# Decode step with two layers: the first dense stage's queries and scores issued key head by key head, half of them as streamed rows

## The chip, the cores and the metric

The kernel runs on one core of one Trainium2 chip. The metric is device time in microseconds, the median of repeated executions. Before the change it is 269.35 us (median of 3 runs, 269.09 to 269.76). A program on the core is five instruction queues: TensorE (PE, with its weight loads shown apart as PEld), VectorE (DVE), ScalarE (ACT), GpSimd (POOL) and SyncE (SP). In this kernel SP does nothing but start DMA transfers, in order, and wait for the room that they need.

## The reference

Four tokens (B = 4, one position each) go twice through attention with a key/value cache and a gated feed-forward block. Cut to what matters:

```python
# D=512, Hq=32 query heads, Hkv=8 key heads, Sk=4096, Dh=128, F=1792, B=4
def attention(x, k_cache, v_cache, wq, wo):
    q = (x @ wq) as [B, Hq, Dh];  k, v repeated 4 times per key head
    p = softmax(q @ k^T * Dh**-0.5)
    return (p @ v) as [B, Hq*Dh] @ wo
def ffn(x, w_gate, w_up, w_down):
    return (gelu(x @ w_gate) * (x @ w_up)) @ w_down
for _ in range(2):
    x = x + attention(layernorm(x), ...)
    x = x + ffn(layernorm(x), ...)
```

Both layers use the same weights and the same caches. A cache tile is 2048 keys of one head of one token, 512 KB; there are 64 key tiles and 64 value tiles, the same for both layers.

## The kernel before, in words

The work goes token by token. `attend_first` does the first attention of token 0. Then, for each token b, the dense stage (out-projection, feed-forward), and then `attend`, which does the second attention of token b together with the first attention of token b+1, so that a tile in SBUF serves what it can. All orders are written out by hand (a manual schedule): each engine runs its instructions in the order of the program, and the framework adds only the waits. All loads go through SP's one queue, and a load is issued when its destination is free and when the transfer eight places earlier has landed.

The eight key heads form two groups of four (GH = 4), `gx` and `gy`; each head has a tile t = 0 and a tile t = 1 (`last`). For each group: queries are projected, "sums" matmuls by slices of the identity (`q_sums_of`, L326) bring them to a layout in PSUM (tile `qe`), DVE spreads them with masks into `qb` (`q_spread`, L334, the instruction at L337), and `scores_of` (L562, matmuls at L568) multiplies them with key tiles. One head's score matmuls write 32 partitions of the tile `sc`, so matmuls of four heads have four places side by side. `soft` (L573) makes the softmax: a reduction (L578), three small DVE steps, ACT's exponential (L590); then `soft_turn` (L596, L598) transposes on DVE, and DVE transposes the key tiles (`Keys.turn`, L513) for the next scores.

Special is the place after the first dense stage (b = 0), class `Early`. Key tiles of the previous attention are still in SBUF. Three first loads for the next token have gone to places that were emptied by copying ("parking") three old tiles elsewhere (L530); these are copied back (L541 on DVE, L544 on POOL, L546 on ACT) when score matmuls have freed other places. `Early.queries` (L1013) projects the 16 query heads of `gx` with matmuls that use weight blocks of `wq_sb` as stationary operand (L258, 4 per query head), into two accumulators in two PSUM banks: heads of key heads 2 and 3, then of 0 and 1. `q_round` (L310, L312) subtracts the mean and rounds to bf16. `Early.scores` (L1045) then runs the scores of `gx` in runs given to `first`, and calls `load` after each, which queues the next key tile for the place that this run frees. `rest` does sums and spread for key heads 0 and 1; `qy` (L1442) projects the 16 query heads of `gy` as streamed rows: 16 matmuls of 512 columns (L286), turned by DVE (L292) and rounded. `build`, called inside `soft`, does their sums and spread, with four matmuls of no use (`busy`, L465) that keep PE occupied.

Of the kernel before, what the change touches and what calls it, by code (L numbers as in the profile page):

```python
# [20 lines left out]
WIDE = 32  # L21
# [14 lines left out]
def kernel(  # L36
# [98 lines left out]
    def wide(v, width=WIDE):  # L135
        n = v.shape[-1]
        return v.unsqueeze(1).broadcast_to([P, width // n, n])
# [119 lines left out]
    def mac(dst, lhsT, rhs, first, last):  # L257
        nc.tensor.matmul(dst, lhsT=lhsT, rhs=rhs, start=first, stop=last, skip_group_check=True)  # L258
# [48 lines left out]
    def q_tile():  # L307
        return grp.tile([P, HG], BF16, name="q_bf", tag="q_bf", bufs=1)
# [9 lines left out]
    def q_sum_tile():  # L318
        return ps_sm.tile([P, GH, BE, rep], FP32, name="qe", tag="sm")
# [675 lines left out]
    class Early:  # L995
# [17 lines left out]
        def queries(self, b, st):  # L1013
            g, half = self.gx, GH // 2
            n = half * rep
            norm = Norm(st)
            norm.root()
            q_bf, qs = q_tile(), []

            def heads(h0, h1):  # L1020
                for i in range(h0, h1):
                    for k in range(KD):
                        mac(qs[-1][:, i % n], wq_sb[g][:, k, i * Dh:(i + 1) * Dh],
                            wide(xb[:, k, :RUN]), k == 0, k == KD - 1)

            qs.append(acc([n, WIDE], "q"))
            heads(n, 2 * n)
            q_round(q_bf, qs[0][:, :, b:b + 1], g, norm, n)
            qs.append(acc([n, WIDE], "q"))
            heads(0, n // 2)  # L1030
            qe = q_sum_tile()
            q_sums_of(qe, q_bf[:], half, half)
            heads(n // 2, n)
            q_spread(qe, half, half)
            q_round(q_bf, qs[1][:, :, b:b + 1], g, norm)

            def rest():
                q_sums_of(qe, q_bf[:], 0, half)
                q_spread(qe, 0, half)
                norm.scales()  # L1040

            self.rest = rest
            return norm

        def scores(self, sc, qy, norm):  # L1045
            gx, gy, own, keys = self.gx, self.gy, self.own, self.keys
            a, c, last = gx * GH, gy * GH, NT - 1

            def home(i, t, freed):
                place[i, t] = own[freed]  # L1050
                return k_tile(i, t).rearrange("p c d -> p (c d)")

            def load(i, t, freed):
                home(i, t, freed)
                assert keys.tile(keys.nl) == (i, t)
                keys.load(1)

            def first(run):
                now = {(a + s, t): place[a + s, t] for s, t in run}
                place.update({k: own[k] for k in now})  # L1060
                scores_of(sc, gx, run)
                place.update(now)

            first([(2, 0), (3, 0)])
            load(a + 3, 0, (a + 2, 0))
            load(a, last, (a + 3, 0))
            self.rest()
            q = qy()
            first([(2, last), (3, last), (0, 0), (1, 0)])
            load(a + 1, last, (a + 2, last))  # L1070
            load(a + 2, last, (a + 3, last))
            to = home(c + 1, last, (a + 1, 0))
            self.one.back(to, 1, nc.vector)
            self.one.back(to, 2, nc.gpsimd)
            self.two[0].back(home(c + 2, last, (a, 0)), 2)
            first([(0, last), (1, last)])
            load(a + 3, last, (a, last))
            to = home(c + 3, last, (a + 1, last))
            self.two[1].back(to, 1)
            other = new_scores()  # L1080

            def build():
                qe = q_sums(q)
                busy(4, other.rearrange("p c j -> p (c j)"))
                q_spread(qe)

            p0 = soft(sc, norm, meanwhile=build)
            self.two[1].back(to, 1, nc.vector)
            return p0, other

    def attend(b, qy, before, norm, early=None):

        gx, gy = second_groups[b - 1]
        prob1, prob2 = {}, {}
        keys = early.keys if early else Keys(b, (gx, gy))
        turn = keys.turn
        kept2, own2, other2, apart2 = two(b - 1)
        kept1, own1, _, apart1 = two(b)
        banks.late = len(apart2)
        vals2 = Values(2, b - 1, kept2 + own2 + apart2, prob2, dst2(b - 1),  # L1100
                       off_ot=len(apart2) > 0)
        late2 = Streamed(b - 1, other2, prob2, dst2(b - 1))
        vals1 = Values(1, b, one(b), prob1, dst1(b), keeps=kept1,
                       streamed=[gy * GH + s for s in range(GH - 1)], park=apart1,
                       sums={4: (ps_sc, "sc"), 5: (ps_sm, "sm"), 6: (ps_sc, "sc")},
                       last_bank=lambda: ps_sm.tile([P, 2, WEIGHT], FP32, name="ot", tag="sm"))

        sc2 = [new_scores(early=True)]
        if early:
            p0, other = early.scores(sc2[0], qy, norm)  # L1110
            sc2.append(other)
        else:
            for t in range(NT):
                scores(sc2[0], gx, t)
                keys.load_pairs(GH // 2)
            before.whole()
            p0 = soft(sc2[0], norm)
            q = qy()
            sc2.append(new_scores())
            busy(4, sc2[1].rearrange("p c j -> p (c j)"))  # L1120
            q_build(q)
        soft_turn(p0)
        ready = 2 if early else 0
        turn(ready)
        for t in range(NT):
            scores(sc2[1], gy, t)
            keys.load(GH)
        ring.extend(1, b, one(b)[ahead_of[b]:])
        ring.extend(2, b - 1, other2)
        ring.extend(2, b, own1)  # L1130
        pe0, den0 = soft_swap(p0, early=True), soft_den(p0)

        def recip():
            prob2[gx] = (pe0, soft_recip(den0))

        p1 = soft(sc2[1], norm, lasting=True, meanwhile=recip)
        vals2.step(2, hold=True)
        qe = q_sums(q1_bf[:, gx, :, b])
        vals2.step(4, hold=True)
        turn()  # L1140
        soft_turn(p1)
        q_spread(qe)
        vals2.flush()
        turn(1 if ready else 2)
        pe1, den1 = soft_swap(p1, early=True), soft_den(p1)
        banks.back_brief()
        banks.back()
        turn()
        prob2[gy] = (pe1, soft_recip(den1))
        turn(0 if ready else 1)  # L1150
        sc1 = new_scores()
        scores(sc1, gx, 0, singly)
        turn(3)
        scores(sc1, gx, 1, singly)
        turn()
        p0 = soft(sc1)
        vals2.step(vals2.left(), hold=True)
        turn()
        soft_turn(p0)
        q_build(q1_bf[:, gy, :, b])  # L1160
        vals2.flush()
        pe, den = soft_swap(p0), soft_den(p0)
        turn()
        prob1[gx] = (pe, soft_recip(den))
        turn()
        vals1.step(2)
        sc1 = new_scores()
        scores(sc1, gy, 0, last_alone)
        turn(4)
        vals1.step(3)  # L1170
        scores(sc1, gy, 1, last_alone)
        p0 = soft(sc1)
        vals1.step(3)
        x = swap_tile()
        busy(5, x.rearrange("p s t c h -> p (s t c h)"))
        vals1.put_aside(1)
        soft_turn(p0)
        vals1.put_aside(1)
        heads = pairs(one(b))
        twice = o1(b)  # L1180
        rows = RowProj(lambda i: twice(i).broadcast_to([P, 2]))
        pe, den = soft_swap(p0, x=x), soft_den(p0)
        vals1.put_aside(0)
        prob1[gy] = (pe, soft_recip(den))
        vals1.put_aside(0)
        vals1.step(2)
        rows.heads(heads[0], hp)
        vals1.step(2)
        rows.heads(heads[1], hp)
        vals1.step(1)  # L1190
        proj = OutProj(o1(b), 1)
        spare = proj.bank[:, KD * WEIGHT:]
        rows.heads(heads[2], rep)
        busy(3, spare)
        vals1.step(1)
        rows.heads(heads[2] + rep, rep)
        rows.split()
        busy(5, spare)
        vals1.step(1)
        proj.heads(heads[3], rep)  # L1200
        vals1.step(1)
        assert vals1.left() == 0
        rows.onto(proj)
        proj.n = Hq - rep
        proj.heads(heads[3] + rep, rep)
        return proj.y, late2
# [276 lines left out]
```

## Time and profile before

| | |
|---|---|
| median of 3 runs | 269.35 us (269.09 to 269.76) |
| the profiled execution, own time | 270.43 us |
| its span, first to last instruction | 268.7 us |
| PE busy | 199.4 us (74%) |
| PEld busy | 126.2 us (47%) |
| DVE busy | 176.4 us (66%) |
| ACT busy | 62.8 us (23%) |
| POOL busy | 3.9 us (1%) |
| DMA | 103.10 MB, mean 384 GB/s |
| mean granted TensorE clock | 0.898 |

How to read it: "busy" is the union of an engine's instructions over the span. The profile's second part cuts the span into 40 slices of 6.7 us and gives for each the busy share in tenths, the granted clock, the DMA share and the rate in GB/s. The chain is the work that ended last, followed back step by step. A timeline row has the start, the length, engine, line, operation, output<-input, and in brackets the idle time before it with what ended it. SPq is SP's queue, where a row is the issue of a transfer and not the transfer.

### The profile page before, as it was taken

The numbers are of one execution on the slowest core, as the hardware profiler recorded it, in microseconds if no ns is written. First come the engines' busy times: TensorE is split into PE (matmuls) and PEld (weight loads), VectorE is DVE, ScalarE is ACT, GpSimd is POOL, SyncE is SP. The second block draws the span as 40 slices with busy tenths as digits, with TensorE's granted clock in tenths as the row PEclk, the third lists the DMA queues.
The fourth block names the chain that finished last, engine by engine and source line by source line (L and its number), as shares of the span: only waits on it lengthen the run. The fifth ranks groups of instructions, "written<-read, shape, count | busy, mean of one in ns | idle before, by whom it ended". The sixth has DMA issues, their size and how long they took to land.

```text
span 268.7 us, 9239 instructions
## 1 busy us (share of the span) xinstructions
PE 199.4 (74%) x4104; PEld 126.2 (47%) x4113; DVE 176.4 (66%) x434; ACT 62.8 (23%) x123; POOL 3.9 (1%) x10
## 2 busy tenths in 40 slices
PE   1395255679689796979689867697699687978884
PEld 1333133568366544547346244364372344654563
DVE  3393952150226899884768997736779986468863
ACT  1001000200404402032315320304235203044630
POOL 2000000000001000000000000000000000000001
PEclk9999559559799978699999988999999977799999
DMA  6999999999996999999999999999999999999940
GB/s 248 420 417 420 417 420 418 413 381 401 409 401 212 396 416 420 417 417 417 395 412 418 417 420 417 417 420 381 395 420 416 417 420 417 417 356 358 417 161 3
DMA packets 32575, 103.10 MB, mean 384 GB/s; under 512 B 2836, under 2 KB 8728, under 8 KB 32536
## 3 DMA queue, kind: packets, MB, share of 16 engines
q1 hardware_dynamic: 32512, 102.51, 95.8%
q8 instruction: 32, 0.52, 0.7%
q14 instruction: 7, 0.06, 0.1%
q10 hardware_dynamic: 24, 0.01, 0.0%
HBM read 102.50 MB, written 0.00 MB: 382 GB/s over the span
## 4 chain that ended last, share of the span: by engine, by line
DMA 44%; PE 26%; DVE 20%; SPq 5%; ACT 2%; issue 2%; DVEq 0%
DMA v_t<-in_A_v_cache_dram 25%; DVE kp L513 11%; DMA kp<-in_A_k_cache_dram 9%; PE sc L568 7%; PE ot L824 6%; DMA wu_sb<-in_B_w_up_dram 5%; DMA kp<-in_A_v_cache_dram 4%; SPq L149 4%; PE y L258 3%; PE so L757 2%; PE u L258 1%; ACT pe L626 1%; PE q L286 1%; DVE pe L578 1%; DVE q L292 1%
## 5 line engine op out<-in xcount | busy, mean ns | idle before, releaser
L513 DVE STREAM_TRANSPOSE kp<-kp 128x1024 f32<-128x1024 f32 x64 | 74.0, 1207 | 0.0
L568 PE MATMUL sc<-kp,qb 128*32 128x512 bf16 x512 | 62.5, 432 | 6.6 <-DVE kp L513 2.2
L824 PE MATMUL ot<-pe,v_t 128*128 128x32 bf16 (+1 forms) x1120 | 37.3, 183 | 16.2 <-DMA v_t<-in_A_v_cache_dram 14.1
L824 PEld LDWEIGHTS <-v_t 128*128 128x128 bf16 x1120 | 34.4, 100 | 25.6 <-DMA v_t<-in_A_v_cache_dram 19.5
L568 PEld LDWEIGHTS <-qb 128*32 128x32 bf16 x512 | 21.8, 100 | 37.4 <-issue 19.3
L590 ACT ACTIVATE pe<-sc,nl 128x512 bf16<-128x512 f32 x8 | 5.5, 687 | 85.5 <-DVE pe L587 76.9
L765 DVE STREAM_TRANSPOSE so<-so 128x256 f32<-128x256 f32 (+1 forms) x19 | 11.1, 586 | 6.1 <-PE so L757 6.1
L623 PE MATMUL x<-pe,ident_bf 128*32 128x128 bf16 x192 | 5.8, 247 | 12.4 <-DVE pe L598 12.2
L258 PEld LDWEIGHTS <-wo_sb 128*128 128x128 bf16 x256 | 12.9, 99 | 3.5 <-DMA wo_sb<-in_A_wo_dram 2.9
L258 PE MATMUL y<-OT_bf,wo_sb 128*128 128x64 bf16 x192 | 11.7, 215 | 2.4 <-DMA wo_sb<-in_A_wo_dram 2.2
L623 PEld LDWEIGHTS <-ident_bf 128*32 128x32 bf16 x256 | 5.4, 102 | 17.1 <-issue 14.8
L578 DVE TENSOR_REDUCE pe<-sc 128x1 f32<-128x512 f32 x12 | 8.3, 690 | 6.3 <-PE sc L568 6.3
L656 DVE TENSOR_TENSOR OT_bf<-ot,rden 128x8 bf16<-128x8 f32 (+1 forms) x20 | 3.0, 156 | 13.5 <-PE ot L824 13.4
L626 ACT CAST pe<-x 128x512 bf16<-128x512 f32 x12 | 7.0, 585 | 20.4 <-PE x L623 20.4
L258 PE MATMUL q<-xb,wq_sb 128*128 128x5 bf16 (+1 forms) x192 | 5.5, 170 | 7.5 <-DMA wq_sb<-in_A_wq_dram 7.5
L757 PE MATMUL so<-v_t,pl 128*32 128x256 bf16 x192 | 9.2, 275 | 2.5 <-DMA v_t<-in_A_v_cache_dram 2.5
L401 DVE TENSOR_TENSOR xb<-XX,y 128x4 bf16<-128x4 f32 (+1 forms) x9 | 1.6, 173 | 13.7 <-PE y L258 13.5
L465 PEld LDWEIGHTS <-ident_bf 128*128 128x128 bf16 x131 | 7.5, 100 | 6.3 <-issue 3.4
L757 PE MATMUL so<-v_t,pe 128*32 128x256 bf16 x192 | 8.9, 303 | 2.1 <-ACT pe L626 1.1
L598 DVE STREAM_TRANSPOSE pe<-pe 128x512 bf16<-128x512 bf16 x12 | 8.4, 697 | 2.0 <-ACT pe L590 2.0
L330 PE MATMUL qe<-q_bf,ident_bf 128*32 128x16 bf16 (+1 forms) x272 | 5.5, 175 | 5.6 <-DVE q_bf L312 2.8
L258 PEld LDWEIGHTS <-wq_sb 128*128 128x128 bf16 x192 | 5.2, 98 | 8.1 <-DMA wq_sb<-in_A_wq_dram 8.1
(152 smaller groups left out, 252.9 us busy)
## 6 DMA issues: line engine op xcount, KB each, us to landing
v_t<-in_A_v_cache_dram SPq DMA_DIRECT2D x97, 512.0 KB, 8.9
kp<-in_A_k_cache_dram SPq DMA_DIRECT2D x56, 512.0 KB, 10.4
wq_sb<-in_A_wq_dram SPq DMA_DIRECT2D x2, 2048.0 KB
wo_sb<-in_A_wo_dram SPq DMA_DIRECT2D x4, 1024.0 KB, 11.4
kp<-in_A_k_cache_dram SPq DMA_DIRECT2D x4, 1024.0 KB, 8.7
wq_sb<-in_A_v_cache_dram SPq DMA_DIRECT2D x3, 1024.0 KB, 12.0
wg_sb<-in_B_w_gate_dram SPq DMA_DIRECT2D x1, 1792.0 KB, 12.5
wu_sb<-in_B_w_up_dram SPq DMA_DIRECT2D x1, 1792.0 KB
```

Source lines behind the costliest of these rows:

```text
L149: dq.dma_start(out=wo_sb[:, i * n:(i + 1) * n], in_=wo_dram[:, i * n:(i + 1) * n])
L258: nc.tensor.matmul(dst, lhsT=lhsT, rhs=rhs, start=first, stop=last, skip_group_check=True)
L465: nc.tensor.matmul(unread, lhsT=ident_bf[:], rhs=rhs[:, :unread.shape[1]], start=start, stop=start, skip_group_check=True)
L513: nc.vector.transpose(out=words, in_=words)
L568: nc.tensor.matmul(sc[s * QS:(s + 1) * QS], lhsT=qb[:, w0:w0 + 2 * W], rhs=kt[:, :, be // 2, :, be % 2], start=(t == 0 and be == 0), stop= ...
L578: nc.vector.tensor_reduce(out=m, in_=sc.rearrange("p c j -> p (c j)"), axis=AX.X, op=ALU.min if norm else ALU.max)
L598: nc.vector.transpose(out=flat, in_=flat)
L623: nc.tensor.matmul(x[a * QS:(a + 1) * QS, s], lhsT=ident_bf[:, s * QS:(s + 1) * QS], rhs=pT[:, a], start=True, stop=True, skip_group_check ...
L626: nc.scalar.copy(out=pe, in_=x.rearrange("p s t c h -> p (s t c h)"))
L757: nc.tensor.matmul(ps[d, :NW * QS], lhsT=x[:, w:w + NW].rearrange("p c h -> p (c h)"), rhs=v[:, i:i + NW, d], start=first and i == 0, stop ...
L765: nc.vector.transpose(out=flat, in_=flat)
L824: nc.tensor.matmul(self.ot[:, s % 2], lhsT=v[:, i, :], rhs=wide(pe[:, s, t * CH + i, :], self.ot.shape[-1]), start=(done == 0 and i == 0), ...
```

## The change

Only `Early.queries`, `Early.scores` and their call are touched.

In `queries`, all 16 query heads of `gx` get one accumulator of 512 columns (one PSUM bank). The heads of key head 2 and those of key head 3 are projected and rounded one key head after the other, and their sums and spreads are issued one key head at a time. The projections by weight blocks of key heads 0 and 1 (32 matmuls) are gone; `other_rows` makes these eight query heads as 16 streamed-row matmuls of 256 columns, and `other_half` turns and rounds them, and does their sums and spread. `norm.root` comes after the first spreads.

In `scores`, the runs of `first` are: (2,0) alone; (2,last) with (3,0); (3,last) alone; (0,0) with (1,0); (0,last) with (1,last). Before they were (2,0) with (3,0); then four together; then (0,last) with (1,last). The loads stand behind the new runs. `other_rows` stands ahead of the run (3,last); `other_half`, the rows of `gy` and their rounding stand ahead of (0,0),(1,0); the sums of `gy` stand ahead of (0,last),(1,last) and its spread, in two halves, behind. One `busy` matmul remains of four. `qy` is no longer called here.

```diff
@@ -1014,35 +1014,33 @@
             g, half = self.gx, GH // 2
             n = half * rep
             norm = Norm(st)
+            q_bf, qe = q_tile(), q_sum_tile()
+            q = acc([2 * n, WIDE], "q")
+            for s in range(half, GH):
+                for h in range(s * rep, (s + 1) * rep):
+                    for k in range(KD):
+                        mac(q[:, h], wq_sb[g][:, k, h * Dh:(h + 1) * Dh], wide(xb[:, k, :RUN]),
+                            k == 0, k == KD - 1)
+                q_round(q_bf, q[:, s * rep:(s + 1) * rep, b:b + 1], g, norm, s * rep)
+            for s in range(half, GH):
+                q_sums_of(qe, q_bf[:], s, 1)
+                q_spread(qe, s, 1)
             norm.root()
-            q_bf, qs = q_tile(), []
-
-            def heads(h0, h1):
-                for i in range(h0, h1):
-                    for k in range(KD):
-                        mac(qs[-1][:, i % n], wq_sb[g][:, k, i * Dh:(i + 1) * Dh],
-                            wide(xb[:, k, :RUN]), k == 0, k == KD - 1)
-
-            qs.append(acc([n, WIDE], "q"))
-            heads(n, 2 * n)
-            q_round(q_bf, qs[0][:, :, b:b + 1], g, norm, n)
-            qs.append(acc([n, WIDE], "q"))
-            heads(0, n // 2)
-            qe = q_sum_tile()
-            q_sums_of(qe, q_bf[:], half, half)
-            heads(n // 2, n)
-            q_spread(qe, half, half)
-            q_round(q_bf, qs[1][:, :, b:b + 1], g, norm)
-
-            def rest():
+
+            def other_rows():
+                steps = [(x, w[:, :n * Dh]) for x, w in q_steps(b, g)]
+                streamed_part(q[:, :n], steps, range(KD))
+
+            def other_half():
+                q_round(q_bf, turn_rows(q[:, :n]), g, norm)
                 q_sums_of(qe, q_bf[:], 0, half)
                 q_spread(qe, 0, half)
                 norm.scales()
 
-            self.rest = rest
+            self.other_rows, self.other_half = other_rows, other_half
             return norm
 
-        def scores(self, sc, qy, norm):
+        def scores(self, sc, b, norm):
             gx, gy, own, keys = self.gx, self.gy, self.own, self.keys
             a, c, last = gx * GH, gy * GH, NT - 1
 
@@ -1061,30 +1059,33 @@
                 scores_of(sc, gx, run)
                 place.update(now)
 
-            first([(2, 0), (3, 0)])
+            first([(2, 0)])
             load(a + 3, 0, (a + 2, 0))
+            first([(2, last), (3, 0)])
             load(a, last, (a + 3, 0))
-            self.rest()
-            q = qy()
-            first([(2, last), (3, last), (0, 0), (1, 0)])
             load(a + 1, last, (a + 2, last))
+            self.other_rows()
+            first([(3, last)])
             load(a + 2, last, (a + 3, last))
+            self.other_half()
+            raw = q_rows(b, gy)
+            q_bf, half = q_tile(), GH // 2
+            q_round(q_bf, turn_rows(raw), gy, norm)
+            first([(0, 0), (1, 0)])
             to = home(c + 1, last, (a + 1, 0))
             self.one.back(to, 1, nc.vector)
             self.one.back(to, 2, nc.gpsimd)
             self.two[0].back(home(c + 2, last, (a, 0)), 2)
+            qe = q_sums(q_bf[:])
             first([(0, last), (1, last)])
+            q_spread(qe, half, half)
             load(a + 3, last, (a, last))
             to = home(c + 3, last, (a + 1, last))
             self.two[1].back(to, 1)
             other = new_scores()
-
-            def build():
-                qe = q_sums(q)
-                busy(4, other.rearrange("p c j -> p (c j)"))
-                q_spread(qe)
-
-            p0 = soft(sc, norm, meanwhile=build)
+            q_spread(qe, 0, half)
+            busy(1, other.rearrange("p c j -> p (c j)"))
+            p0 = soft(sc, norm)
             self.two[1].back(to, 1, nc.vector)
             return p0, other
 
@@ -1107,7 +1108,7 @@
 
         sc2 = [new_scores(early=True)]
         if early:
-            p0, other = early.scores(sc2[0], qy, norm)
+            p0, other = early.scores(sc2[0], b - 1, norm)
             sc2.append(other)
         else:
             for t in range(NT):

```

## The prediction

> **What bounds the kernel now.** I read the page's rates by slice and its chain first, then SP's waits, then the stage that the change touches, row by row.
>
> ```profile
> GB/s 248 420 417 420 417 420 418 413 381 401 409 401 212 396 416 420 417 417 417 395 412 418 417 420 417 417 420 381 395 420 416 417 420 417 417 356 358 417 161 3
> DMA 44%; PE 26%; DVE 20%; SPq 5%; ACT 2%; issue 2%; DVEq 0%
> ```
>
> 103 MB have to come in, and nearly every slice runs at 395 to 420 GB/s: the span is the transfers plus a start and a tail. The one hole is slice 13 (80.6 to 87.3 us) at 212, and it is the changed stage. Seen closer, in stretches of 1 us (the last number is GB/s):
>
> ```profile
> 81.00:82.00 1.00, 1.00 (x40) 0.81 (x39) 0.47 (x2) 0.05 (x1) 0.00 (x0) 1.00 0.46 188
> 82.00:83.00 1.00, 1.00 (x32) 0.64 (x31) 0.05 (x1) 0.00 (x0) 0.00 (x0) 1.00 0.12 49
> 83.00:84.00 1.00, 1.00 (x26) 0.71 (x20) 0.59 (x4) 0.00 (x0) 0.00 (x0) 1.00 0.29 53
> ...
> 125.00:130.00 5.00, 4.00 (x132) 2.59 (x128) 3.75 (x14) 3.19 (x5) 0.00 (x0) 1.00 1.00 393
> ```
>
> SP's waits tell why: it stood 8.4 us at one key load, put down to PE, until the first run of scores had freed a place.
>
> ```profile
> SPq L494 <- PE qe L330: 8.8, 2, 8.4
> ```
>
> So an earlier first load is worth its full length, as long as nothing behind it gets late. Behind it is the second thing to see, the chain of this stretch: it is all compute from 78 to 114 us, DVE without a pause from 89 (5.00 us busy of 5 in 95 to 100), and the chain meets a transfer again at 114.
>
> ```profile
> 85.71 1.94 ACT kp L546 x2
> 87.64 0.77 ACT pe L590 x2
> 88.42 0.02 issue
> 88.44 0.58 DVE pe L598
> 89.02 0.06 issue
> 89.08 2.33 DVE kp L513 x2
> ...
> 114.00 6.94 DMA v_t<-in_A_v_cache_dram
> ```
>
> The softmax's exponential (87.52) waits for ACT's three copies, and these wait for the scores of heads 0 and 1.
>
> **The change, step by step.** Prices come from these rows:
>
> ```profile
> 79.74 1.35 PE L258 MATMUL q<-xb,wq_sb 128*128 128x32 bf16 x48
> 80.73 0.22 DVE L312 SCALAR_TENSOR_TENSOR q_bf<-cs_q,ln,q 128x8 bf16<-128x8 f32 x1 [0.21 <-PE q L258]
> 81.02 0.27 PE L330 MATMUL qe<-q_bf,ident_bf 128*32 128x8 bf16 x16
> 81.37 0.29 DVE L337 TENSOR_TENSOR qb<-qe,masks 128x128 bf16<-128x128 f32 x1 [0.41 <-PE qe L330]
> 81.71 0.63 PE L568 MATMUL sc<-kp,qb 128*32 128x512 bf16 x4
> ```
>
> A projection matmul lasts 0.176 and follows the last by 0.025; 16 sums take 0.27; a round of score matmuls starts 0.233 after the last one whether one, two or four places are filled, and lands 0.39 after its start. Hand-overs are 0.08 (PE to DVE), 0.07 and 0.05 (DVE to PE).
>
> 1. *First load.* Head 2's 16 projections end at 80.29, its rounding at 80.53. The compiled order of the changed kernel marks the first projection of head 3 as waiting for DVE, and so the first sum of head 3, while the score matmuls of (2,0) behind it carry no wait of their own. I read this as follows: PE may not write the query bank while DVE reads it, nor the sums' bank while DVE spreads. Then the heads do not overlap: projections of head 3 80.60 to 81.15, rounding to 81.39, head 2's spread 81.40 to 81.64 (0.24, an estimate from 0.29 for 128 columns and 0.41 for 256), head 3's sums from 81.70, scores (2,0) from 81.82 in four lone rounds to 82.91. The load goes at 82.94, and went at 82.84: **+0.1**. If head 3 need not wait, the same sum gives 82.37: **-0.45**. These are the two ends; I take +0.1, because the marked waits say so.
>
> The Trainium skill, "PSUM — Partial Sum Buffer", in its section on bank collisions, speaks against the change: two engines must not touch one bank in the same 32 partitions at once, even at other columns, so waits go by bank. Before, the halves had a bank each; no run here has yet shown the shared case. By the page the sum is +0.1, without it -0.45.
>
> 2. *The other loads.* (2,last) and (3,0) run 82.75 to 83.85: loads at 83.88 and 84.30 (83.27 and 84.73 before). Streamed rows end at 84.31 (four rounds of half of 0.216 each), (3,last) at 85.24: load at 85.27 (85.15).
>
> 3. *Heads 0 and 1 are late.* Before, their spread was ready at 83.33. Now: transpose of 256 columns 0.46 (the so row of that size at L765), rounding, sums, spread, ready at 85.78; the 16 rows of gy (0.87 before, all ahead of the scores in PE's queue) run 85.26 to 86.30. Scores (0,0),(1,0) run 86.13 to 87.22, and before were done at 84.71: **+2.5**. As a check: 12 rounds of scores become 20, so 8 x 0.233 = 1.9; 32 projections less give back 0.8, rows of 256 columns cost 0.43, and the rest is the DVE round trip.
>
> 4. *What hangs on it.* ACT's copies start 2.5 later (84.80 to 87.31). DVE: turn of gy 86.35, rounding to 87.34, the copy back to 88.07 (0.69), two spreads to 88.68; PE's gy sums wait for that rounding, so (0,last),(1,last) end at 88.62; then reduction and three small steps to about 90.2. Exponential at 90.3 and not 87.52: **+2.75**. Scores of gy start at 88.73 (86.66). Loads six and seven go at 88.65 and 89.82 (85.62 and 87.75). Three busy matmuls less win nothing: PE waits there anyway. Root and scales have room to the exponential.
>
> 5. *Out to the stream.* DVE has no pause from 89 to 112, so +2.75 arrives at 114. The next waits of PE for value tiles, at 120.98 and 122.27, give back some 0.5: the dense stage of token 1 is **+2.3**. Does this matter, when the stream is the bound? It does once loads come so late that too little is queued. Bytes issued less bytes landed, read from the trace at each issue, are 3.9 us of transfers at 110.38, 4.1 at 114.00, 3.7 at 118.19, and only 2.6 at 125.62; then 2.6 to 3.4 until 135. The chain shows one of these: 5.94 us from issue at 127.87 to the end of the wait. A lone transfer needs 2.7 to 3.3 us from issue to landing (the load of 82.84 landed at 85.57 to 86.10). So transfers of 1.25 us need about 3.5 us between issue and mean landing. With issues 2.3 late, those of 125.62 to 134.29 (4.1 to 5.1 from issue to mean landing before, so 0.6 to 1.6 spare) get short by 0.7 to 1.7, less some 0.3 where a wait of PE for a tile goes away (0.44 at 130.97). At 110 and 118 I count 0.5 to 0.9, which is the same lateness and not added. Between 0.7 and 1.7 I take 1.2, and 0.1 from step 1: **+1.3 us**. After 135 the queue holds 7 to 9 us again, and PE waits for tiles at 155 to 176, so the compute's lateness dies there and the stream's stays.
>
> The Trainium skill, "DMA: Bandwidth & Descriptors", section on the anatomy of one DMA, gives a fixed 2.0 us plus bytes at 436 GB/s, 3.2 us for a tile (fitted on another issue path). The 2.7 to 3.3 here is near; with 3.2 for 3.5 the sum would be +1.0.
>
> The profiled execution took 270.43 (268.7 span and 1.7 around it), so it would take 271.7; it lies 1.1 above the median of the runs, so the median goes from 269.35 to **270.65**.
>
> **The rivals.** About 0.3% (0.8 us) is what a measurement of this kernel can tell from no change.
>
> - *A, forecast:* late compute eats the queue's lead. +0.8 to +2.0, 270.1 to 271.4. Chance 0.58.
> - *B, the queue covers it:* the late compute costs nothing since 2.6 us are queued at the thinnest place; only the restart counts, +0.1 to +0.6, 269.65. For it: no slice between 90 and 230 falls below 381 now. Against it: at 2.6 us queued, 125 to 130 already runs at 393. Chance 0.20.
> - *C, faster:* head 3's projections do not wait, the first load goes at 82.37 (-0.45), and the late compute, then some 2.2, is covered. The earlier queue can also win part of what 84 to 90 lose now with little queued (315, 279, 326 and 391 GB/s against 417: 1.1 us): -0.9, 268.45. It decides where the first load is issued before 82.6 and over 1.5 us stay queued at 126. Against it: the marked waits. Chance 0.08.
> - *D, the whole lateness:* the chain from 78 to 114 is all compute; if the stream waits for every late issue, 2.75 less 0.5 stays: +2.3, 271.6. For it: the chain. Against it: 4.1 us queued at 114. Chance 0.14.
>
> **How the numbers follow.** A and D are slower by over 0.3%, except A's low edge (0.02); B is no change; of C 0.06 is faster and 0.02 is not: faster 0.06, same 0.24, slower 0.70. The range leaves out C and the upper half of D, 0.15 in all: 269.3 to 271.8.
>
> **What would show it.** First load near 82.94 and not 82.4 (step 1); head 3's projections after a pause of 0.3 at 80.3; ACT's first copy near 87.3 and the exponential near 90.3 (steps 3, 4); rates of 125 to 140 below 393 to 408 (step 5). I am wrong if those rates hold (B), if the first load is early (C), or if PE's clock, 1.0 from 75 to 90 now, drops in the new pauses, which I leave out.

## The result and the profile after

The changed kernel is slower. Its median is 273.0 us (6 runs, 270.74 to 275.92) beside 269.56 for the kernel before on the same chip (269.09 to 271.17): ratio 1.0102, 95% interval 1.0067 to 1.0138, or +1.8 to +3.7 us. Timed a second time, unchanged (x13 below), it gave 1.0071 (1.0045 to 1.0096). Both fit +1.8 to +2.6 us. The ratios here leave out executions more than 1.5% above the fastest of their kernel: the 275.92 among these six, and three of the twelve of x12. The first profiled execution took 272.78 (span 271.0, mean clock 0.884), the second 272.01 (270.2, 0.899), and that of before 270.43.

The rates by slice and the engines' shares of the chain, from the page of the changed kernel:

```profile
GB/s 253 420 418 420 418 420 417 409 383 404 406 389 183 288 399 418 417 408 390 394 398 418 418 417 415 423 415 404 391 415 416 417 421 417 418 384 393 417 164 3
DMA 45%; PE 23%; DVE 19%; SPq 8%; issue 2%; ACT 1%; DVEq 0%
```

The hole in slice 13 (183) is deeper than before (212), and slice 14 has become a second hole (288 for 396). Slices 18 to 21 (408 390 394 398) are the next dense stage, a little slower than 417 417 395 412. Slice 36 went the other way, 384 for 356. SP's longest wait in the stage is now for scores and 0.5 longer (8.4 before; the three numbers are the total in us, how often, and the longest):

```profile
SPq L494 <- PE sc L568: 16.7, 9, 8.9
```

The stage itself, in the timeline of the changed kernel; the brackets hold the idle time ahead of a row and what ended it:

```profile
79.57 0.55 PE L258 MATMUL q<-xb,wq_sb 128*128 128x32 bf16 x16
80.16 0.22 DVE L312 SCALAR_TENSOR_TENSOR q_bf<-cs_q,ln,q 128x4 bf16<-128x4 f32 x1 [0.25 <-PE q L258]
80.43 0.55 PE L258 MATMUL q<-xb,wq_sb 128*128 128x32 bf16 x16 [0.31 <-DVE q_bf L312]
...
81.53 0.26 PE L330 MATMUL qe<-q_bf,ident_bf 128*32 128x4 bf16 x16 [0.36 <-DVE qb L337]
81.66 2.05 PE L568 MATMUL sc<-kp,qb 128*32 128x512 bf16 x8
83.31 13.03 SPq L494 DMA_DIRECT2D kp<-in_A_k_cache_dram  x13
...
88.58 2.84 ACT L546 COPY kp<-park 128x1024 bf16<-128x1024 bf16 x3 [5.64 <-PE sc L568]
91.63 0.78 ACT L590 ACTIVATE pe<-sc,nl,ln 128x512 bf16<-128x512 f32 x1 [0.20 <-DVE pe L587]
```

Both pauses that step 1 read from the marked waits are there: PE stood 0.31 until DVE had rounded head 2's queries out of the shared bank, and 0.36 until DVE had spread out of the sums' bank. But the first load went at 83.31 and the exponential at 91.63, later than forecast (the dense stage ended 0.17 earlier here than in the trace of before). The windows of this trace say why; the number behind the five busy times is the granted clock:

```profile
81.00:82.00 1.00, 0.64 (x34) 0.41 (x35) 0.57 (x3) 0.00 (x0) 0.00 (x0) 0.97 0.48 197
82.00:83.00 1.00, 1.00 (x7) 0.36 (x5) 0.38 (x3) 0.41 (x2) 0.00 (x0) 0.50 0.11 33
83.00:84.00 1.00, 1.00 (x14) 0.35 (x12) 0.00 (x0) 0.00 (x0) 0.00 (x0) 0.50 0.00 0
84.00:85.00 1.00, 1.00 (x15) 0.38 (x14) 0.00 (x0) 0.00 (x0) 0.00 (x0) 0.50 0.49 131
```

From 82 to 85.4 PE had half its clock: rounds of score matmuls start 0.43 us apart there, and 0.22 apart in the second profile of the same kernel, which had no such stretch:

```profile
82.00:83.00 1.00, 1.00 (x14) 0.72 (x14) 0.48 (x3) 0.36 (x2) 0.00 (x0) 1.00 0.16 57
83.00:84.00 1.00, 1.00 (x22) 0.69 (x17) 0.00 (x0) 0.05 (x1) 0.00 (x0) 1.00 0.08 16
84.00:85.00 1.00, 0.73 (x14) 0.14 (x12) 0.69 (x2) 0.00 (x0) 0.00 (x0) 1.00 0.85 270
```

There the timeline is the forecast one. Its dense stage ended 0.06 earlier than that of before, so add 0.06 to compare: first load 82.88 (forecast 82.94), ACT's copies 87.05 (87.31), exponential 90.15 (90.3).

```profile
80.54 0.55 PE L258 MATMUL q<-xb,wq_sb 128*128 128x32 bf16 x16 [0.31 <-DVE q_bf L312]
...
82.82 11.66 SPq L494 DMA_DIRECT2D kp<-in_A_k_cache_dram  x13
...
86.99 2.84 ACT L546 COPY kp<-park 128x1024 bf16<-128x1024 bf16 x3 [3.94 <-PE sc L568]
...
90.09 0.78 ACT L590 ACTIVATE pe<-sc,nl,ln 128x512 bf16<-128x512 f32 x1 [0.26 <-DVE pe L587]
```

So the second profile is the one to account by. Where the bytes were lost, in windows of before and then of the second profile (last number GB/s):

```profile
86.00:88.00 2.00, 1.93 (x25) 0.63 (x28) 1.77 (x7) 2.00 (x3) 0.03 (x1) 1.00 0.91 326
88.00:90.00 2.00, 1.69 (x31) 0.77 (x28) 1.56 (x2) 1.05 (x4) 0.00 (x0) 1.00 1.02 391
90.00:92.00 2.00, 0.96 (x32) 0.94 (x32) 2.00 (x4) 0.25 (x1) 0.00 (x0) 1.00 1.03 408
92.00:95.00 3.00, 2.38 (x96) 2.19 (x96) 2.86 (x11) 1.18 (x3) 0.00 (x0) 0.99 1.02 407
130.00:135.00 5.00, 3.73 (x100) 1.94 (x92) 3.39 (x14) 0.41 (x2) 0.00 (x0) 1.00 1.02 406
```

```profile
86.00:88.00 2.00, 1.77 (x36) 0.64 (x30) 1.76 (x4) 1.01 (x2) 0.95 (x2) 1.00 0.77 242
88.00:90.00 2.00, 1.91 (x24) 0.55 (x20) 1.49 (x7) 1.83 (x3) 0.22 (x1) 1.00 1.01 410
90.00:92.00 2.00, 1.33 (x32) 0.55 (x29) 1.66 (x5) 1.18 (x3) 0.00 (x0) 1.00 0.93 332
92.00:95.00 3.00, 1.70 (x65) 1.47 (x52) 2.97 (x6) 0.59 (x1) 0.00 (x0) 1.00 0.97 300
130.00:135.00 5.00, 3.52 (x112) 2.14 (x105) 3.42 (x12) 2.03 (x3) 0.00 (x0) 1.00 0.95 320
```

From 86 to 95, 2 x 84 - 2 x 19 + 2 x 76 + 3 x 107 = 603 KB less arrive, 1.45 us at 417 GB/s. From 130 to 135 it is 5 x 86 = 430 KB, 1.0 us. What the stream lost in this profile it lost at these two places and a little between 115 and 125 us: it is 1.45 late at its 36th MB, still 1.7 at its 46th, and 2.9 at its 54th (138 us in the kernel before). The rest of the account is in the page of the second profile:

```profile
GB/s 251 422 416 420 419 418 418 410 382 403 408 392 202 338 403 417 417 407 409 338 401 418 416 417 419 415 420 397 398 415 419 416 419 418 418 399 395 419 149 3
```

Slices 36 and 37 (236 to 250 us) run at 399 and 395, before at 356 and 358: 80 GB/s over 6.75 us is 540 KB, **1.3 us won back** at the end.

### The profile page after: what moved, and what is told of

Its sections match the earlier page's. It is cut to its first block, busy times and chain, and to the rows that moved or that the text cites. A ratio compares the mean times of both kernels' runs of the same rounds, so it can differ in the third digit from the quotient of the medians.

```text
span 271.0 us, 9246 instructions
## 1 busy us (share of the span) xinstructions
PE 202.2 (75%) x4110; PEld 125.4 (46%) x4110; DVE 177.0 (65%) x438; ACT 62.9 (23%) x123; POOL 3.9 (1%) x10
## 4 chain that ended last, share of the span: by engine, by line
DMA 45%; PE 23%; DVE 19%; SPq 8%; issue 2%; ACT 1%; DVEq 0%
DMA v_t<-in_A_v_cache_dram 25%; DMA kp<-in_A_k_cache_dram 12%; DVE kp L513 10%; PE sc L568 7%; PE ot L824 5%; DMA kp<-in_A_v_cache_dram 4%; SPq L149 4%; DMA wd_sb<-in_B_w_down_dram 4%; SPq L154 3%; PE y L258 3%; PE so L757 2%; PE q L286 2%; DVE q L292 1%; DVE pe L578 1%; SPq L150 1%
## 5 line engine op out<-in xcount | busy, mean ns | idle before, releaser
L568 PE MATMUL sc<-kp,qb 128*32 128x512 bf16 x512 | 67.4, 443 | 5.9 <-DVE kp L513 1.9
L568 PEld LDWEIGHTS <-qb 128*32 128x32 bf16 x512 | 23.2, 102 | 38.8 <-issue 20.8
L578 DVE TENSOR_REDUCE pe<-sc 128x1 f32<-128x512 f32 x12 | 8.3, 689 | 5.9 <-PE sc L568 5.9
L258 PE MATMUL q<-xb,wq_sb 128*128 128x5 bf16 (+1 forms) x160 | 4.8, 169 | 7.8 <-DMA wq_sb<-in_A_wq_dram 7.5
L286 PE MATMUL q<-wq_sb,xb 128*32 128x512 bf16 (+1 forms) x128 | 10.0, 380 | 0.3 <-DVE xb L401 0.3
L292 DVE STREAM_TRANSPOSE q<-q 128x512 f32<-128x512 f32 (+1 forms) x8 | 5.6, 697 | 7.0 <-PE q L286 7.0
L757 PE MATMUL so<-v_t,pe 128*32 128x256 bf16 x192 | 8.0, 274 | 2.8 <-ACT pe L626 1.4
```

Source lines behind the costliest of these rows:

```text
L286: nc.tensor.matmul(flat[j * QS:(j + 1) * QS], lhsT=x.broadcast_to([P, WIDE]), rhs=blocks[:, j], start=i == 0, stop=i == len(steps) - 1, sk ...
L292: nc.vector.transpose(out=flat, in_=flat)
L568: nc.tensor.matmul(sc[s * QS:(s + 1) * QS], lhsT=qb[:, w0:w0 + 2 * W], rhs=kt[:, :, be // 2, :, be % 2], start=(t == 0 and be == 0), stop= ...
L578: nc.vector.tensor_reduce(out=m, in_=sc.rearrange("p c j -> p (c j)"), axis=AX.X, op=ALU.min if norm else ALU.max)
L757: nc.tensor.matmul(ps[d, :NW * QS], lhsT=x[:, w:w + NW].rearrange("p c h -> p (c h)"), rhs=v[:, i:i + NW, d], start=first and i == 0, stop ...
```

## The experiments

The theory after the result: lateness of the stage's compute reaches the stream, which is the bound, wherever SP's queue is thin, and at more places than the one that I priced. The rivals: the new waits and the half clock behind them; the streamed rows as such; the eight extra rounds of scores. All runs on the same table: how late the exponential of the stage is (or VectorE behind it), and how late the stream has landed its 36th MB (94.38 us in before), its 54th (138.23) and its 102.4th (258.02). All are in us, from one profile each, and shifted so that the first dense stage ends at 79.40 in every trace. One profile is one execution: the row of x14, which costs nothing that its interval shows, moves by +0.5 and -0.9. The ratio comes from 5 to 12 runs beside the kernel before on the same chip.

| kernel | exponential late | 36th MB | 54th | 102.4th | ratio (95%) |
|---|---|---|---|---|---|
| changed, first profile (half clock) | 4.28 | 2.79 | 3.75 | 2.22 | 1.0102 (1.0067 to 1.0138) |
| x13_after_again | 2.63 | 1.45 | 2.90 | 1.40 | 1.0071 (1.0045 to 1.0096) |
| x1_two_banks | 2.16 | 0.16 | 1.86 | 1.79 | 1.0064 (1.0036 to 1.0093) |
| x2_filled | 2.79 | 1.69 | 2.88 | 1.63 | 1.0079 (1.0046 to 1.0111) |
| x3_late | 2.79 | 1.27 | 2.58 | 1.31 | 1.0082 (1.0050 to 1.0114) |
| x4_heads_together | 2.52 | 1.01 | 2.30 | 0.83 | 1.0114 (1.0078 to 1.0150) |
| x5_runs_only | 0.92 | 0.38 | 0.33 | 0.42 | 0.9992 (0.9967 to 1.0017) |
| x6_rows_only | 1.44 | 2.02 | 3.11 | 1.96 | 1.0092 (1.0059 to 1.0125) |
| x8_dve_late | 0, VectorE 2.4 | -0.18 | 2.82 | 1.78 | 1.0072 (1.0051 to 1.0094) |
| x9_lone_first (half clock) | 1.87 | 1.99 | 1.92 | 0.55 | 1.0001 (0.9982 to 1.0021) |
| x10_no_rows | 1.77 | 1.43 | 2.06 | 0.93 | 1.0073 (1.0043 to 1.0103) |
| x11_dve_later | 0, VectorE 5.04 | 0.25 | 4.63 | 2.89 | 1.0138 (1.0111 to 1.0164) |
| x12_dve_half | 0, VectorE 1.45 | -0.34 | 2.89 | 1.19 | 1.0032 (1.0000 to 1.0063) |
| x14_dve_early | 0, VectorE -2.3 | -0.09 | 0.50 | -0.91 | 1.0015 (0.9992 to 1.0039) |
| x15_no_rows_in_time | 2.84 | 1.66 | 2.57 | 0.87 | 1.0089 (1.0061 to 1.0116) |
| x16_after_dve_early (half clock) | 4.25, VectorE 2 | 3.13 | 4.42 | 3.39 | 1.0096 (1.0063 to 1.0130) |

**x1_two_banks**, from the changed kernel: no waits on the query bank.

```diff
...
+            q2 = acc([rep, WIDE], "q")
+            q = acc([n + rep, WIDE], "q")
...   # key head 2 is projected into q2, key head 3 into q[:, n:]
```

> The changed kernel, with the queries of key head 2 in a PSUM bank of their own, so that the projections of key head 3 need not wait for the rounding of key head 2 on DVE. If the shared query bank is what delays the first load and opens the first pause of PE: pause of 0.3 us at 80.4 gone, first load some 0.3 us earlier than in the changed kernel in clock-equal stretches. Theory 'pauses lower the clock': the granted clock stays 1.0 up to 90 us, the time falls to 270.0 to 271.0. Theory 'late compute alone': the time falls only by about 0.3, to 272.5.

```profile
79.85 0.95 PE L258 MATMUL q<-xb,wq_sb 128*128 128x32 bf16 x32
...
81.35 0.26 PE L330 MATMUL qe<-q_bf,ident_bf 128*32 128x4 bf16 x16 [0.36 <-DVE qb L337]
...
82.53 0.34 SPq L494 DMA_DIRECT2D kp<-in_A_k_cache_dram  x1
```

The 32 projections are one run of 0.95, the first pause is gone and that of the sums' bank stays. The load goes at 82.42 (this trace's dense stage ends 0.11 late), near the forecast's other end, 82.37. What the stage lost is nearly gone with it: the 36th MB is 0.16 late, and 1.45 in x13. Yet the ratio is +0.64%, beside +0.71% in x13: with the exponential 2.2 late the stream loses 1.7 more by its 54th MB.

**x2_filled**, from the changed kernel: matmuls of no use fill PE's pauses.

```diff
+                if s > half:
+                    busy(1, spare)
+                    busy(1, spare[:, :256])   # ahead of head 3's projections
...
+                if s > half:
+                    busy(2, spare)            # ahead of head 3's sums
```

> The changed kernel, with four matmuls of no use (512, 256, 512 and 512 columns, into the bank that the scores will clear) in the two places where PE stands waiting for DVE, ahead of the projections of key head 3 and of its sums. No wait is taken away and no other order changed. Theory 'pauses lower the clock': no half clock between 78 and 90 us, scores of heads 2 and 3 at 0.233 a round, first load near 82.9 to 83.1, exponential near 90.4, time 270.3 to 271.0, runs closer together. Theory 'late compute alone' (the clock falls by chance or for another reason): as the changed kernel, 272 to 273.5.

The half clock did not fall into the stage. The exponential came within 0.1 of the forecast and the loads within 0.4. The cost stayed at +0.79%.

**x3_late**, from the kernel before: lateness, by a split of the second run of scores (four rounds more) and nine matmuls of no use ahead of the scores of heads 0 and 1.

```diff
...
-            first([(2, last), (3, last), (0, 0), (1, 0)])
+            first([(2, last), (3, last)])
             load(a + 1, last, (a + 2, last))
             load(a + 2, last, (a + 3, last))
+            busy(9, self.spare)
+            first([(0, 0), (1, 0)])
```

> The kernel before, with the scores of heads 2 and 3 at t = last in a run of their own and then nine matmuls of no use of 448 columns, so that scores of heads 0 and 1 end 2.5 to 2.8 us later than before while the first four loads go when they did and PE has no pause. It prices step 5 of the forecast alone. Step 5 as forecast: +0.7 to +1.7 us, 270.1 to 271.2. If the queue covers late compute: +0.3 at most, 269.8. If all lateness stays: +2.2 or more, 271.7.

The exponential is 2.79 late, the first four loads are on time (within 0.02), the fifth and sixth go 2.9 and 3.0 late, and the kernel costs +0.82%, as much as the change. So late compute, with the loads that hang on it, is enough for the whole effect; the projections, sums and streamed rows here are those of the kernel before.

**x4_heads_together**, from the changed kernel: heads 2 and 3 in one projection, one rounding, one set of sums, one spread.

```diff
...
-            for s in range(half, GH):
-                q_sums_of(qe, q_bf[:], s, 1)
-                q_spread(qe, s, 1)
+            q_sums_of(qe, q_bf[:], half, half)
+            q_spread(qe, half, half)
```

> The changed kernel without its pipeline by key head: the projections of key heads 2 and 3 go together, with one rounding, one set of sums and one spread, as before; runs of scores, streamed rows and loads as changed. Neither pause of the pipeline is there. Theory 'pauses lower the clock': clock 1.0 up to 86 us, first load near 82.7, exponential near 90.2, time 270.0 to 271.0. Theory 'late compute alone': the same order of lateness and so the same time as the changed kernel at equal clock, 272 to 273.

```profile
81.16 0.27 PE L330 MATMUL qe<-q_bf,ident_bf 128*32 128x8 bf16 x16 [0.31 <-DVE q_bf L312]
81.84 1.26 PE L568 MATMUL sc<-kp,qb 128*32 128x512 bf16 x8 [0.42 <-DVE qb L337]
```

The pauses between the heads are gone, but others stand in their place, against what was expected: PE waits 0.31 ahead of the common sums and 0.42 ahead of the first scores, about as long in all as in the changed kernel. The exponential is still 2.52 late, the clock stays whole in the stage, and the kernel costs +1.14%. So the order head by head is not what costs. This run does not take PE's waits away; x3 does, with no wait of PE from 79 to 87 us, and costs as much.

**x5_runs_only**, from the kernel before: the changed runs of scores and their loads.

```diff
-            first([(2, 0), (3, 0)])
+            first([(2, 0)])
             load(a + 3, 0, (a + 2, 0))
+            first([(2, last), (3, 0)])
...
+            first([(3, last)])
...
+            first([(0, 0), (1, 0)])
```

> The kernel before with the changed runs of scores alone ((2,0); (2,last) with (3,0); (3,last); (0,0) with (1,0); (0,last) with (1,last)) and the loads behind them; projections as before. Eight rounds of scores more, 1.9 us, all ahead of heads 0 and 1 but for the last four: scores of heads 0 and 1 end some 1.0 to 1.4 us late. Theory 'late compute stays in the stream nearly whole': +0.6 to +1.2, 270.6 to 271.2. Forecast's step 5 (queue gives 1.0 back): 0 to +0.3, 269.9.

The eight extra rounds (8 x 0.233 = 1.9 us of PE) make the exponential 0.92 late and the fifth and sixth load 1.0 and 1.1, and cost nothing that can be seen: 0.9992 (-0.9 to +0.5 us). When these two loads were issued, 3.3 and 3.1 us of transfers were still queued.

**x6_rows_only**, from the kernel before: heads 0 and 1 as streamed rows.

```diff
...
+                steps = [(x, w[:, :n * Dh]) for x, w in q_steps(b, g)]
+                streamed_part(qs[1], steps, range(KD))
+                q_round(q_bf, turn_rows(qs[1]), g, norm)
```

> The kernel before with the streamed rows for key heads 0 and 1 alone; runs of scores and the projections of key heads 2 and 3 as before. First load 0 to 0.2 us earlier (16 projections less ahead of it), heads 0 and 1 late by the round trip over DVE (transpose, rounding, sums, spread), which nothing covers since the second run needs them: 1.3 to 1.8 us. Theory 'late compute stays nearly whole': +0.8 to +1.5. Forecast's step 5: +0.2 to +0.5.

+0.92% with an exponential only 1.44 late. Here the third to fifth load go 1.44 late too (86.17 for 84.73) at the start of the hole, where 1.2 us were queued instead of 2.1, and the 36th MB is already 2.0 late.

**x8_dve_late**, from the kernel before: two more transposes on DVE behind the exponential and behind the loads of the stage.

```diff
         soft_turn(p0)
+        if early:
+            kvh, t = keys.tile(keys.nt)
+            words = k_tile(kvh, t).rearrange("p c d -> p (c d)").bitcast(FP32)
+            for _ in range(2):
+                nc.vector.transpose(out=words, in_=words)
```

> The kernel before with two more transposes of one key tile on DVE (they undo each other) right behind the first softmax's transpose, at 89 us: DVE is 2.4 us later from there on, but all scores and loads up to the thirteenth of the stage go when they did. It tells the two places apart in which lateness can meet the queue. Theory 'the queue is short at loads six and seven (85 to 92 us)': this lateness costs little, 0 to +0.9. Theory 'the queue is short at the next dense stage (119 to 136 us)': +1.5 to +2.4, as much as in the run with late scores.

Two of its windows:

```profile
92.00:95.00 3.00, 0.05 (x5) 0.05 (x8) 2.98 (x5) 0.00 (x0) 0.00 (x0) 0.99 1.03 412
...
130.00:135.00 5.00, 3.25 (x112) 2.05 (x104) 2.85 (x10) 1.52 (x3) 0.00 (x0) 1.00 0.97 359
```

The first eight loads go within 0.1 us of their old times, there is no new hole at 86 to 95 (350, 385, 391 and 412 GB/s for 326, 391, 408 and 407), and still it costs +0.72%. The stream loses 3.0 between its 36th and its 54th MB, from 114 us up to and in the dense stage of the next token: that is the second way, on its own.

**x9_lone_first**, from the kernel before: the lone run (2,0) over two query banks, with as many rounds of scores as before.

```diff
...
+            first([(2, 0)])
             load(a + 3, 0, (a + 2, 0))
+            self.more()    # head 3's sums and spread, the projections of heads 0 and 1
             self.rest()
             q = qy()
+            first([(2, last), (3, 0), (0, 0), (1, 0)])
...
```

> A version that keeps what the change wants and not its price: key heads 2 and 3 one by one with two query banks, heads 0 and 1 projected by weight blocks as before, and runs (2,0); (2,last),(3,0),(0,0),(1,0) together; (3,last),(0,last),(1,last) together, 12 rounds as before. First load at 82.4 to 82.6, the next at 84.7, heads 0 and 1 late by 0.2 to 0.5. Theory 'a load is worth its length only with the next one close behind': 0 to +0.3. Theory 'the first load is worth its full length': -0.3 to -0.4, 269.6.

1.0001, as the first theory had it. But its profile caught the half clock at 81.4 and is the longest of its twelve executions (271.34, median 270.31), so its first load (83.40) says little of the others. Whether an early first load alone would pay stays open.

**x10_no_rows**, from x5_runs_only: heads 2 and 3 one by one as well; no rows.

```diff
...
+            for s in range(half, GH):
+                q_sums_of(qe, q_bf[:], s, 1)
+                q_spread(qe, s, 1)
+                heads((s - half) * n // 2, (s - half + 1) * n // 2)
```

> The change without its streamed rows: heads 2 and 3 go key head by key head, with the changed runs of scores, but heads 0 and 1 are projected by weight blocks, as before, into a second bank; their rest and rounding stand ahead of the rounds of heads 0 and 1. Theory R (the cost is the way of the streamed rows over VectorE, which makes heads 0 and 1 late): nothing is turned back, so the time is 0 to +0.3% beside before (269.5 to 270.8). Rival P (the pipeline and its runs cost too, once they stand together): +0.5% or more.

+0.73%: the theory that the rows are the cost fell. But the projections of heads 0 and 1 now stood ahead of the first scores, the first load went at 83.63 (0.8 late), and the exponential was 1.77 late. To part these, later:

**x15_no_rows_in_time**, from x10_no_rows: these 32 projections go into `rest`.

```diff
...
             def rest():
+                heads(0, n)
+                q_round(q_bf, qs[1][:, :, b:b + 1], g, norm)
```

> As x10_no_rows, but the 32 projections of heads 0 and 1 stand behind the runs of scores of heads 2 and 3, so that the first load goes near 82.9 and not 83.6; the exponential should stay 1.3 to 1.8 late. Theory L (what counts is how late VectorE's chain is): +0.3 to +0.7%, as x10_no_rows. Rival F (x10_no_rows paid for its late first load): +0.2% or less.

The first load is on time (82.98), the exponential 2.84 late, more than I expected, and the cost +0.89%. No streamed row of heads 0 and 1 is in it, and it costs what the change costs at the same lateness. So neither a late first load nor these rows are needed for the cost.

**x11_dve_later** and **x12_dve_half** have four transposes, or two of half a tile, in place of x8's two.

> As x8_dve_late (two extra transposes of a key tile on VectorE behind the first half's softmax, 2.4 us, which cost +0.72%), with four of them, 4.8 us. Theory L (lateness of VectorE at this point beyond some 0.9 us goes through to the end nearly one for one): +3.7 to +4.5 us, +1.4 to +1.7%. Rival S (the stream loses one hole and no more): +2.0 to +2.5 us, +0.7 to +0.95%.

> As x8_dve_late, with two transposes of half a tile, some 1.2 to 1.3 us. Theory L (lateness beyond some 0.9 us goes through nearly one for one): +0.2 to +0.5 us, +0.1 to +0.2%. Rival W (all lateness on VectorE behind this point goes through, and what covered 0.9 us in x5_runs_only was something else): +0.9 to +1.2 us, +0.35 to +0.45%.

DVE is 5.04 late in the one (four of 1.26) and 1.45 in the other. They cost 3.7 us (3.0 to 4.4) and 0.9 (0.0 to 1.7), and x8 in between 1.9 (1.4 to 2.5). The price grows with the lateness and does not stop at one hole; of each lateness 0.5 to 1.3 stays covered (1.45 - 0.9, 2.4 - 1.9, 5.04 - 3.7). x11 speaks for L and against S; x12's interval holds the forecasts of both L and W. Where it is lost moves with the lateness: in x11 the stream loses 4.2 of its 4.6 between its 42nd and 46th MB (109 to 118 us in before), a place where x8 loses about 1.

**x13_after_again** is the changed kernel.

> The changed kernel again, for a second profile and more times: 271.5 to 273.5, +0.8 to +1.3%. Whether the half clock falls into the stage again: if it is granted at 82 to 85 again, the first exponential of the stage is near 91.8 (set by the weights' end at 79.40, as in the first profile); if the clock is whole there, near 90.3, as the forecast and x2_filled have it. If the times with and without it lie within 0.3% of each other, the half clock is not what the forecast missed.

Full clock in the stage, exponential at 90.15, 272.01 and a median of 272.19. The profiled executions with and without the half clock, 272.78 and 272.01, differ by 0.28%, so by the bound set beforehand the half clock is not what the forecast missed.

**x14_dve_early** (from the kernel before) and **x16_after_dve_early** (from the changed one) leave two transposes out.

```diff
-        turn(ready)
+        if early:
+            keys.nt += ready
```

> The kernel before without the first two transposes of key tiles behind the first half's softmax in the stage (2.33 us of VectorE; the scores of these tiles are of keys that are not transposed). Theory Q (VectorE's chain has some 0.9 us of slack here and does not bound the kernel before): 0 to -0.2%. Rival B (the chain from 78 to 114 us bounds the kernel, so that what makes it earlier is gained): -1.0 to -2.0 us, -0.4 to -0.75%.

From x14's chain, and one row of its timeline:

```profile
100.63 9.79 DMA v_t<-in_A_v_cache_dram
...
112.79 8.86 DMA v_t<-in_A_v_cache_dram
```

```profile
115.43 0.69 DVE L530 TENSOR_SCALAR park<-v_t 128x512 int32<-128x512 int32 x1 [0.42 <-DMA v_t<-in_A_v_cache_dram]
```

+0.15%, which is no change. The chain of this stretch, compute up to 114 us in before, is now two long transfers with 2.4 us of PE between them, and DVE, ahead of time, waits 0.42 for a transfer. In the kernel before, DVE's chain and the stream are in balance here: later costs, earlier gives nothing that this interval (0.9992 to 1.0039) shows.

> The changed kernel without the first two transposes of key tiles behind the first half's softmax in the stage (2.33 us of VectorE, as in x14_dve_early), so that VectorE's chain is only some 0.4 us late behind them, while the loads of 84 to 92 us stay as late as the change makes them. Theory L (the lateness goes to the stream by VectorE's chain): 0 to +0.2%. Rival Q (the late loads themselves cost, 1.0 to 1.4 us by the 36th MB): +0.4 to +0.6%.

+0.96%: nothing came back, and the cost lies above what either theory had. Its profile caught the half clock twice in this stretch, and PE then took DVE's place:

```profile
99.45 0.51 PE L623 MATMUL x<-pl,ident_bf 128*32 128x128 bf16 x12 [1.94 <-issue]
99.89 0.61 PE L603 MATMUL den<-zx,masks 128*128 128x16 f32 x2
100.43 5.48 PE L568 MATMUL sc<-kp,qb 128*32 128x512 bf16 x32
```

DVE's next reduction (L578) starts at 105.95, after a wait of 0.68 for these score matmuls, and in the first profile of the changed kernel at 105.98. So the profile cannot part the two: DVE was some 2 us ahead of that profile only up to there, and as late behind it. What it does show is that the hole of the stage is not made by DVE behind the exponential: the 36th MB is 3.1 late here, 2.8 in that profile. Whether late loads alone would be enough for the whole cost stays open. What two profiles show side by side is firmer: x8 loses only from 114 us on, x13 loses 1.45 by its 36th MB and another 1.45 by its 54th.

## Why the prediction was wrong

It said +1.3, 270.65; measured are 273.0 and 272.19, by the ratios +2.7 and +1.9 us. Both times lie above its range of 269.3 to 271.8; put on the 269.35 of the kernel before, the ratios give 272.1 and 271.3, and the second of these lies inside. The direction was right.

- *Step 1, first load +0.1.* Right. 82.88 for 82.94 at full clock, both pauses as marked; with two banks 82.42. The 0.31 that PE waits with one bank and not with two agree with the Trainium skill, "PSUM — Partial Sum Buffer", section on bank collisions: accesses are kept apart by bank, though the columns differ. x1 took another tile along with another bank, so it does not part a wait by bank from a wait by tile.
- *Steps 2 to 4, the timeline.* Right within 0.3 at full clock (x13, x2), but for two loads: the one behind (3,last) went at 84.77 for 85.27 in x13, the third at 84.68 for 84.30 in x2. What I left out, the clock in the pauses, took 1.6 more in the first profile (exponential 4.28 late for 2.63).
- ***Step 5, out to the stream, is the step that failed.*** It looked for thin places of the queue only from 110 us on, though step 4 had loads six and seven (counted from 82.84 they are the fifth and sixth) 3.0 and 2.1 late. Those of 85.62 and 87.75 had found 3.8 and 3.6 us of transfers queued; those of the second profile at 88.37 and 89.86 found 2.0 and 1.8. That hole cost 1.45 by the 36th MB, where I had 0.1. Looking there would not have been enough: these two loads had 6.2 and 5.4 us from issue to mean landing before, so the rule of 3.5 would have priced them at 0.2 to 0.4; in the second profile the sixth took 4.5. The dense stage, which I put at 1.2 of a possible 0.7 to 1.7, cost another 1.45. And "the stream's stays" was wrong the other way: 1.3 was won back at 236 to 250 us, where the kernel before itself runs at 356 and 358 GB/s. In the account of one execution the errors nearly cancel: 1.45 + 1.45 - 1.3 = 1.6, and 272.01 - 270.43 = 1.58, so that the 271.7 forecast for it came near by luck.
- *The carry to the median.* The forecast 270.65 stood on the 269.35 of three runs. Beside x13 the kernel before itself had a median of 270.33, so of the 1.5 us by which 272.19 lies above the forecast 1.0 is not the change's. By the ratios the forecast +1.3 is 0.6 too low for the second timing, within its interval (+1.2 to +2.6), and 1.4 too low for the first, below its interval (+1.8 to +3.7). One execution is one draw: that of before lay 1.1 above its median, those of the changed kernel 0.2 below theirs, and the medians of the kernel before, measured beside these kernels, ran from 269.56 to 270.4.
- *Rivals.* D (+2.3, "the whole lateness") is nearest to what both timings fit: with 2.4 to 2.85 late, the 54th MB is 2.3 to 2.9 late. But D has neither the hole in the stage nor the gain at the end, so its size is in part luck, and the second timing's +1.9 lies in A's band as well. B, that the queue covers it, holds up to 0.9 (x5) and not at 2.5. C had its early load in x1 and gained nothing, since the lateness behind it was not covered. x14 adds that an earlier VectorE chain wins nothing here.
- *Open.* How often the half clock falls into the stage, and what it takes from the median: the intervals around 1.0102 and 1.0071 overlap, and x2, with the pauses filled, costs as much as the change. The account of one execution, 1.6, lies inside the second timing's interval and below the first's; what made the first timing longer is not shown. x6 costs more than its 1.44 by the table's trend (1.6 to 3.4 us), and x9 less; I can't say why.

## What to carry to other kernels

When a stream is the bound, price a late stage at every place where issued less landed falls to about a lone transfer's round trip (2.7 to 3.3 us here), starting with the stage's own loads, and ask at the end where the stream has holes that give some back. Here 0.9 us of lateness was covered, and more went through for most of its length (x6 and x9 stand apart); making the same chain earlier gave nothing. Compare medians taken side by side: the kernel before alone moved by 0.8 us between them.

## What the runs showed of the hardware

The granted clock halved for 3.4 us or multiples of it (3.4 to 17.1 in these traces, each a multiple of 3.413 but for the last one of a trace), and the same kernel with the same pauses had such a stretch at 82 us in one profile and none in the other. In each trace all changes of the clock lie on one grid of 3.413 us, and the place of the grid differs from run to run: near this stage a point of the grid lies at 81.94 in the first profile and at 83.00 in the second. The Trainium skill, "TensorE: Matmul & The Clock Gate", Part 1, has a free-running window of about 3.4 us over which PE's activity is watched; both observations agree with it. How much idleness is enough is not shown. By the matmul records PE was busy 0.77 of the window ahead of the stretch in the first profile, and 0.81 of the window up to 83.00 in the second, which kept its clock; but in x9 a stretch followed a window with 0.94, at 81.6 us of that trace, and in x6 none followed one with 0.76, at 86.7. That the pauses caused the stretch is not shown either: x9 had it in a stage with other pauses, and x4, with pauses of about the same length in all, had none.
